# Full-attention layers: a lower cap on side products, a shorter hold on the side bank, and one PSUM read for each bank of keys and queries

## Chip, cores and metric

One core of a Trainium2 chip runs the whole program. The metric is the device time of one execution in microseconds (us). The engines work in parallel and are tied by semaphores: TensorE (PE, matrix products), ScalarE (ACT), VectorE (DVE), GpSimd (POOL), and the queue of SyncE (SP), which issues most DMAs. Products land in banks of PSUM; PE, ACT and DVE reach those banks, POOL works on SBUF only.

## What is computed

Four transformer layers on x of 2048 tokens by 512 features, 32 heads of 16. Layers 0 and 2 attend to a sliding window of 256 keys (weights A), layers 1 and 3 to all 2048 keys, unmasked (weights B):

```python
qkv = (x @ wqkv).reshape(B, S, 3, H, Dh)               # S=2048, H=32, Dh=16
scores = einsum("bhqd,bhkd->bhqk", q, k) * Dh ** -0.5  # A: masked outside 0 <= i-j < 256
o = einsum("bhqk,bhkd->bhqd", softmax(scores), v) @ wo
x = x + A(layernorm(x)); x = x + B(layernorm(x))       # and both once more
```

## The kernel before, in words

**Main work of a full layer.** The layer (1 or 3) has 512 steps. A step is one tile of 128 keys against 512 queries for four heads (`attn_full`). Four groups of eight "quads" of heads and 16 key tiles make 4 x 8 x 16 steps in layer 1; layer 3 runs in the order t (four pairs of quads), c (four chunks of queries), two quads, 16 tiles, so that one (t, c) section has 32 steps. In each step `exps` (L695) issues four score products (L703) into two score tiles and two exponentials on ACT (L707), each over 128x1024. There are three score tiles in PSUM, used in turn. Two steps later `pv` (L747) multiplies the exponentials by the values into the bank `acc[0]`. After the 16 tiles of a quad `epilogue` (L662) has DVE transpose that bank (L670, then short instructions to L687).

**Side work.** Everything else that PE has to do runs as products slipped in after the `pv` of a step: keys and queries of the next chunks or layers (`project`, L472), values (`values`), and the output projection with the residual (`wo`, `wo_part`). In a full layer all of it accumulates in one bank, `acc[1]` (`bank`, L373). A *unit* is one accumulation in that bank: 12 products for a tile of keys, queries, values or `wo`, 12 of half width for half a tile of values, three for `wo_part` (L642). Each product is four 32-column matmuls (L395). PE's instructions are in the order in which Python emits them; the other engines are ordered by the scheduler of the framework, with raised priority where the code says `high_priority`.

**Who decides how much.** `Side.share` (L919) is called once a step, after the `pv`. It adds to `budget`, at least `least` (0.33 or 0.34 in layer 1 and in t = 0, 1 of layer 3; zero later, where the work left over the steps left is what counts), limits it to 0.75, and issues products of 0.222 each while budget, `lag` and the gate allow it. The gate is `clock[0] >= PH["free"]`: `clock` is a planned time that moves by 0.27 for each `exps` (two a step), 1.0 for each `pv`, 0.222 for each product, and by at least 1.8 from step to step. At the end of a unit `mms` (L383) sets `PH["free"]` to the clock plus `after`: 1.6 in general, 2.2 for the units of `project`.

**What follows a unit of keys or queries.** DVE writes the rounded half `sp[:, 0]` (fp16, L508) and the rest `sp[:, 1]` (L509), both from the bank; POOL squares the first half (L514); the SP queue stores both (L519 to L523). When the last unit of the work is done, `keys` or `queries` puts a closure on `pend`: sums of the squares over each head by a product with `hsum` (`squares`, L528, the matmul in L532), again in `acc[1]`, then a maximum (L548) or a scaled copy (L561, L565) by DVE. The next `mms` of any side work empties `pend` first (`settle`, L570), closes the gate for 1.6, and gives the step back. `key_shift` (L575) empties it too, without closing the gate.

Of the kernel before, what the change touches and what calls it, by code (L numbers as in the profile page):

```python
# [9 lines left out]
F32 = mybir.dt.float32  # L10
# [9 lines left out]
P = 128  # L20
NT = S // P
NC = D // P
HT = P // DH
NHT = H // HT
QC = 512
# [6 lines left out]
MM = 0.222  # L32
HEAD_START = 100
EB, XB, XNB, WB, VB, OB = 6, 6, 4, 2, 3, 5
# [155 lines left out]
def fast_path(ctx, tc, flag, a_x, a_wqkv, a_wo, b_wqkv, b_wo, out):  # L190
# [3 lines left out]
    nc = tc.nc  # L194
# [3 lines left out]
    vp = pool("work", 2)  # L198
# [12 lines left out]
    XC, XN, V, O, OT, KM, PH = {}, {}, {}, {}, {}, {}, {"free": 0.0}  # L211
    WT, ST, SP, pend = {}, {}, {}, []

    clock, DONE, XNR, ONR = [0.0], {}, {}, {}
# [6 lines left out]
    def spent(us):  # L221
        clock[0] += us
        return us

    def wait(us):

        return "wait", clock[0] + us
# [124 lines left out]
    def weights(ty, s, n, f0=0, f1=D):  # L352

        for k in ((ty, s), n):
            if k in WT:
                return WT[k].pop() if len(WT[k]) > 1 else WT.pop(k)[0]
        w = wp.tile([P, NC, 2, D], F16, name=f"w{n}", tag="w", bufs=WB)
        if f1 - f0 == D:
            nc.sync.dma_start(w, wd[ty, s])
        else:  # L360
            nc.sync.dma_start(w[:, :, :, :f1 - f0], wd[ty, s][:, :, :, f0:f1])
        return w
# [10 lines left out]
    def bank():  # L373

        if PH["full"]:
            return acc[1]
        turn["bank"] += 1
        PH["extra"] += 1
        if turn["bank"] % 2 and not PH["win"]:
            return ps_s.tile([P, 2, QC], F32, name=f"bs{turn['bank']}", tag="s")[:, 0, :]  # L380
        return PH["pool"].tile([P, QC], F32, name=f"b{turn['bank']}", tag="b")

    def mms(ps, pairs, after=1.6, us=MM, go=True):  # L383


        if PH["full"] and pend:
            settle()
            PH["free"] = clock[0] + 1.6
            yield 0.1
        if PH["win"]:  # L390
            PH["unit"], PH["extra"] = PH["now"], 0
        for i, (a, b) in enumerate(pairs):
            if PH["full"]:
                for g in range(0, P, 32):
                    nc.tensor.matmul(ps[g:g + 32], a[:, g:g + 32], b, start=(i == 0), stop=(i == len(pairs) - 1),  # L395
                                     skip_group_check=True)
            else:
                nc.tensor.matmul(ps, a, b, start=(go and i == 0), stop=(i == len(pairs) - 1))  # L398
            spent(us)
            if i < len(pairs) - 1:  # L400
                if PH["full"]:
                    yield us
                elif i % PH["run"] == PH["run"] - 1:
                    yield PH["run"] * us
            else:
                PH["free"], PH["unit"] = clock[0] + after, None
    TERMS = ((0, 0), (0, 1), (1, 0))
# [64 lines left out]
    def project(l, s, c, act, ht=None, first=False):  # L472


        ty, n = l % 2, f"{l}_{s}_{c}" + ("" if ht is None else f"_h{ht}")
        here = n in WT or (ty, s) in WT
        w = weights(ty, s, n, *((0, D) if ht is None else (ht * P, (ht + 1) * P)))
        yield wait(0 if here else 8)
        xc = XC[l, c]
        if s == 0:  # L480
            dst = rows(qs[ty, c])
        elif ty == 0:
            dst = rows(kw[c])
        else:
            dst = rows(kf)[:, :, c * QC:(c + 1) * QC]
        sqs, begun = {}, []
        if first:
            for t in range(NHT):
                begun.append(bank())
                for k in range(NC):  # L490
                    nc.tensor.matmul(begun[t], w[:, k, 0, t * P:(t + 1) * P], xc[:, 0, k, :], start=(k == 0), stop=False)
                    spent(MM)
        for t in range(NHT) if ht is None else (ht,):
            w0 = t * P if ht is None else 0
            if first:
                ps = begun[t]
                yield from mms(ps, [(w[:, k, a, w0:w0 + P], xc[:, b, k, :]) for a, b in TERMS[1:] for k in range(NC)], go=False)
            else:
                ps = bank()
                yield from mms(ps, [(w[:, k, a, w0:w0 + P], xc[:, b, k, :]) for k in range(NC) for a, b in TERMS], 2.2)  # L500
            settle(not sqs)
            sp = vp.tile([P, 2, QC], F16, name=f"sp{n}_{t}", tag="sp", bufs=4)
            e = 1.0 / UP[s]
            with tc.high_priority(HEAD_START):
                if act:
                    nc.scalar.activation(sp[:, 0], ps, AF.Copy, scale=e)
                else:
                    nc.vector.tensor_scalar(sp[:, 0], ps, e, None, op0=ALU.mult)  # L508
                LAST["DVE"] = nc.vector.scalar_tensor_tensor(sp[:, 1], ps, e, sp[:, 0], op0=ALU.mult, op1=ALU.subtract).ins  # L509
            sq = vp.tile([P, QC], BF16, name=f"sq{n}_{t}", tag="sq", bufs=NHT)  # L510
            if act:
                nc.scalar.activation(sq, sp[:, 0], AF.Square)
            else:
                nc.gpsimd.tensor_tensor(sq, sp[:, 0], sp[:, 0], ALU.mult)  # L514
            sqs[t] = sq

            d = dst[8 * t:8 * t + 8].rearrange("h (d b) n -> (h d) b n", b=4)
            if s:
                nc.sync.dma_start(d[:, 0:2], sp[:, 0:1].broadcast_to([P, 2, QC]))  # L519
                last = nc.sync.dma_start(d[:, 2], sp[:, 1])  # L520
            else:
                nc.sync.dma_start(d[:, 0:2], sp)
                last = nc.sync.dma_start(d[:, 2], sp[:, 0])  # L523
            LAST["SP"] = last.ins
            yield -MM if PH["full"] else -PH["run"] * MM
        return sqs
# [12 lines left out]
    def keys(l, c, act, ht=None, first=False):  # L539
        sqs = yield from project(l, 1, c, act, ht, first)  # L540

        def rest():
            ph = squares(f"k{l}_{c}_{ht}", sqs)
            if l not in KM:
                KM[l] = vp.tile([P, NQ], F32, name=f"km{l}", tag="km", bufs=2)
            r = quarters(ht)
            with tc.high_priority(HEAD_START):
                nc.vector.tensor_reduce(KM[l][r, c:c + 1], ph[r], axis=AX.X, op=ALU.max)  # L548
        pend.append((clock[0] + 3.6, rest, None))
# [20 lines left out]
    def settle(all_=True, most=9):  # L570
        while pend and most and (all_ or pend[0][0] <= clock[0]):
            pend.pop(0)[1]()
            most -= 1
# [13 lines left out]
    def values(l, c, act, halves=(0, 1), tiles=range(4)):  # L587
# [17 lines left out]
        for i in tiles:  # L605
            ps = bank()[:, :D1 - D0]
            yield from mms(ps, [(xc[:, b, k, i * P:(i + 1) * P], w[:, k, a, :D1 - D0]) for k in range(NC) for a, b in TERMS], us=us)
            src = ps.rearrange("p (h d) -> p h d", d=DH)
            for x, h in enumerate(halves if l % 2 else (None,)):
                to = vt[:, i, :, :DH] if h is None else dst[h][:, i, :, :DH]  # L610
                fr = src if h is None else src[:, x * HH:(x + 1) * HH]
                if act:
                    nc.scalar.activation(to, fr, AF.Copy)
                else:
                    LAST["DVE"] = nc.vector.tensor_copy(to, fr).ins  # L615
                one = vt[:, i] if h is None else dst[h][:, i]
                if act:
                    nc.scalar.activation(one[:, :, DH:], one[:, :, :1], AF.Copy, scale=0.0, bias=1.0)
                else:
                    nc.gpsimd.tensor_scalar(one[:, :, DH:], one[:, :, :1], 0.0, 1.0, op0=ALU.mult, op1=ALU.add)  # L620
            yield -us if PH["full"] else -PH["run"] * us
# [228 lines left out]
    class Side:  # L850
# [67 lines left out]

        def share(self):  # L919

            self.budget = min(self.budget + max((self.cost - self.spent) / max(self.steps - 3 - self.k, 1), self.least), 0.75)
            self.lag = max(self.lag - max(0.29, self.least), -0.3)
            while self.q and clock[0] >= PH["free"] and self.budget >= MM / 2 and (self.lag < 0.25 or self.budget > 0.45):
                c = self.one()
                if c is None:
                    break
                self.budget -= abs(c)
                self.lag += abs(c)
# [290 lines left out]
```

## Time and profile before

| | us |
|---|---|
| median of 3 runs (2687.54 to 2692.13) | 2688.03 |
| the profiled execution | 2687.51 |
| its span, first to last instruction | 2685.7 |
| PE busy / ACT busy / DVE busy / POOL busy | 2596.8 / 2390.2 / 844.9 / 580.7 |
| layer 1 (first to last `pv` product) | 454.6 to 1408.8 |
| layer 3 (the same) | 1722.4 to 2671.8 |

The granted clock of PE is 0.995 on average. A busy share says only that an engine had something in flight: both PE and ACT overlap consecutive instructions, so the pitch at which instructions start or end is the measure used below. Rows of the timeline give start, duration, engine, line, operation, tiles, count of merged instructions, and in brackets the idle time before with what ended it.

### The profile page before, as it was taken

Reading aid. Unit: us, or ns where it says so; the run is one execution under the profiler, and the core shown is the slowest. Engines: PE = TensorE matmul, PEld = TensorE weight load, DVE = VectorE, ACT = ScalarE, POOL = GpSimd, SP = SyncE. Lnnn points to the kernel's source line nnn. Section 1 sums busy time; section 2 is a strip of 40 time slices with the busy share of each in tenths; the row PEclk is TensorE's granted clock in tenths of the full one; section 3 lists DMA queues with packets and bytes.
Section 4 is the critical chain, followed back from the end, with each engine's and each line's share of the span. In section 5 each row is a group of like instructions: output and inputs, shape, how many; then the busy total and the mean of one; then the engine's idle time right before and its main releaser. Section 6 shows DMA issues by size and latency. Waiting matters only on the chain.

```text
span 2685.7 us, 59504 instructions
## 1 busy us (share of the span) xinstructions
PE 2596.8 (97%) x24337; PEld 753.9 (28%) x24337; DVE 844.9 (31%) x1937; ACT 2390.2 (89%) x2747; POOL 580.7 (22%) x1203
## 2 busy tenths in 40 slices
PE   8999999999999999999999999999999999999998
PEld 3333344322222222222223333422222222222221
DVE  5746653112232223111216656211222212121111
ACT  5777655999999999999997777699999999999997
POOL 1889750000000000000007777000000000000000
PEclk9999999999999999999999999999999999999999
DMA  6978765223343234222326665423334333333331
GB/s 206 232 219 252 225 204 175 64 95 111 100 101 101 99 111 113 85 68 88 103 76 200 174 182 152 141 82 96 117 123 123 114 106 110 107 101 119 99 93 49
DMA packets 294636, 343.72 MB, mean 128 GB/s; under 512 B 110080, under 2 KB 200672, under 8 KB 289360
## 3 DMA queue, kind: packets, MB, share of 16 engines
q1 hardware_dynamic: 285840, 312.77, 38.8%
q0 software_dynamic: 8512, 27.04, 3.5%
q8 instruction: 193, 3.16, 0.5%
q14 instruction: 91, 0.75, 0.1%
HBM read 228.07 MB, written 96.99 MB: 121 GB/s over the span
## 4 chain that ended last, share of the span: by engine, by line
PE 80%; ACT 8%; DVE 5%; issue 4%; DMA 2%; POOL 1%; SPq 0%; ACTq 0%; DVEq 0%
PE acc L747 31%; PE s L703 21%; PE b L398 11%; PE acc L395 10%; ACT e L707 7%; PE acc L781 5%; PE bs L398 2%; DVE ot L670 1%; DMA wo<-wd 1%; DMA x<-in_A_x_dram 1%; DVE wa L330 0%; DVE sp L509 0%; PE acc L532 0%; DVE xh L437 0%; DVE xh L443 0%
## 5 line engine op out<-in xcount | busy, mean ns | idle before, releaser
L707 ACT ACTIVATE e<-s 128x1024 f32<-128x1024 f32 (+2 forms) x2432 | 2245.5, 1115 | 127.3 <-PE s L703 110.7
L747 PE MATMUL acc<-e,vt 128*17 128x512 f32 x8192 | 1078.8, 598 | 7.9 <-DVE ot L670 6.9
L703 PE MATMUL s<-qt,kt 64*128 64x512 f16 (+3 forms) x5504 | 768.5, 355 | 33.2 <-ACT e L707 16.7
L703 PEld LDWEIGHTS <-kt 64*128 64x128 f16 x5504 | 198.4, 94 | 773.2 <-issue 754.6
L773 POOL TENSOR_SCALAR_AFFINE_SELECT e<-e 128x256 f32<-128x256 f32 x512 | 231.7, 461 | 67.3 <-ACT e L707 66.4
L747 PEld LDWEIGHTS acc<-e,vt 128*17 128x17 f32 x8192 | 136.3, 95 | 387.5 <-issue 352.1
L670 DVE STREAM_TRANSPOSE ot<-acc 128x512 f32<-128x512 f32 x128 | 91.3, 713 | 438.4 <-PE acc L747 324.5
L770 POOL TENSOR_SCALAR_AFFINE_SELECT e<-e 128x256 f32<-128x256 f32 x448 | 198.7, 450 | 50.4 <-ACT e L707 46.2
L781 PE MATMUL acc<-e,vt 128*17 128x384 f32 (+2 forms) x2816 | 195.8, 389 | 0.5 <-POOL e L773 0.5
L687 POOL TENSOR_TENSOR oh<-o,oh 128x512 f16<-128x512 f32 x31 | 36.0, 1163 | 703.6 <-DVE oh L686 703.6
L398 PE MATMUL b<-xc,w 128*128 128x512 f16 x676 | 161.9, 382 | 5.4 <-DVE sp L509 3.7
L514 POOL TENSOR_TENSOR sq_h<-sp_h 128x512 bf16<-128x512 f16 x27 | 28.1, 1041 | 439.2 <-DVE sp_h L508 439.2
L395 PE MATMUL acc<-xc,w_h 128*32 128x512 f16 x1296 | 108.5, 379 | 2.3 <-DVE km L548 2.3
L514 POOL TENSOR_TENSOR sq<-sp 128x512 bf16<-128x512 f16 x28 | 29.1, 1041 | 375.6 <-DVE sp L508 346.0
L395 PE MATMUL acc<-xc,w 128*32 128x512 f16 x1344 | 108.9, 379 | 0.0
L508 DVE TENSOR_SCALAR sp_h<-acc 128x512 f16<-128x512 f32 x27 | 18.6, 690 | 285.4 <-PE acc L395 285.4
L508 DVE TENSOR_SCALAR sp<-acc 128x512 f16<-128x512 f32 x28 | 19.3, 689 | 280.3 <-PE acc L395 270.0
L653 DVE SCALAR_TENSOR_TENSOR x<-acc,x 128x512 f32<-128x512 f32 x60 | 41.5, 692 | 206.9 <-PE acc L395 203.9
L398 PEld LDWEIGHTS <-w 128*128 128x128 f16 x800 | 71.9, 98 | 113.9 <-issue 37.7
L395 PE MATMUL acc<-wo,oh 128*32 128x512 f16 x1296 | 101.3, 379 | 1.3 <-DVE m_None L565 1.3
L615 DVE COPY vt<-acc 128x256 f32<-128x256 f32 (+1 forms) x36 | 18.5, 514 | 258.7 <-PE acc L395 258.7
L395 PE MATMUL acc<-wv,xc 128*32 128x256 f16 (+1 forms) x1728 | 93.2, 308 | 0.2 <-DVE km L548 0.2
(145 smaller groups left out, 1625.8 us busy)
## 6 DMA issues: line engine op xcount, KB each, us to landing
kt<-kf SPq DMA_DIRECT2D x128, 512.0 KB
xd<-x SPq DMA_DIRECT2D x96, 256.0 KB
qt<-qs SPq DMA_DIRECT2D x96, 256.0 KB
x<-xd SPq DMA_DIRECT2D x96, 256.0 KB
w<-wd SPq DMA_DIRECT2D x16, 1024.0 KB
qs<-sp SPq DMA_DIRECT2D x48, 256.0 KB
wo<-wd SPq DMA_DIRECT2D x10, 1024.0 KB
wv<-wd SPq DMA_DIRECT2D x17, 512.0 KB
```

The costliest lines, as they stand in the source:

```text
L395: nc.tensor.matmul(ps[g:g + 32], a[:, g:g + 32], b, start=(i == 0), stop=(i == len(pairs) - 1), skip_group_check=True)
L398: nc.tensor.matmul(ps, a, b, start=(go and i == 0), stop=(i == len(pairs) - 1))
L508: nc.vector.tensor_scalar(sp[:, 0], ps, e, None, op0=ALU.mult)
L514: nc.gpsimd.tensor_tensor(sq, sp[:, 0], sp[:, 0], ALU.mult)
L653: nc.vector.scalar_tensor_tensor(xs[i], ps, 1.0 / (UP[2] * UP[3]), xs[i], op0=ALU.mult, op1=ALU.add)
L670: nc.vector.transpose(ot.rearrange("p b r -> p (b r)"), a)
L703: nc.tensor.matmul(ps[:, h, s0:s0 + wd_], kt[R * h:R * h + R, pr, kc:kc + P], qt[R * h:R * h + R, pr, qc:qc + wd_], start=True, stop=True)
L707: LAST["ACT"] = nc.scalar.activation(e[:, :, w0:w1], ps[:, :, w0:w1], AF.Exp, scale=SCALE).ins
L747: nc.tensor.matmul(a[32 * h:32 * h + DH + 1, :], V[l, qd // 4, j // 8][:, j % 8, 4 * (qd % 4) + h, :], es_[h // 2][:, h % 2, :], start=(j ...
L770: last = nc.gpsimd.affine_select(v, v, pattern=[[0, 2], [-1, P]], compare_op=ALU.is_gt, fill=0.0, base=0, channel_multiplier=1)
L773: last = nc.gpsimd.affine_select(v, v, pattern=[[0, 2], [1, P]], compare_op=ALU.is_ge, fill=0.0, base=0, channel_multiplier=-1)
L781: nc.tensor.matmul(a[32 * h:32 * h + DH + 1, q * P:(q + nb) * P], V[l, (4 * c + j) // 4][:, j % 4, 4 * qd + h, :], es_[h // 2][:, h % 2, s ...
```

## The change

In full layers `share` limits the budget to 0.55 in place of 0.75; every unit closes the gate for 1.45 in place of 1.6 or 2.2, and a `settle` in `mms` as well; and `project` copies the bank into an SBUF tile first (fp32, from the ring of six buffers that also holds x and other 128x512 fp32 tiles), from which L508 and L509 then read. In sliding-window layers the copy is not made, and neither the gate nor the cap is used.

```diff
-    def mms(ps, pairs, after=1.6, us=MM, go=True):
+    def mms(ps, pairs, after=1.45, us=MM, go=True):
         if PH["full"] and pend:
             settle()
-            PH["free"] = clock[0] + 1.6
+            PH["free"] = clock[0] + 1.45
             yield 0.1
...
                 ps = bank()
-                yield from mms(ps, [(w[:, k, a, w0:w0 + P], xc[:, b, k, :]) for k in range(NC) for a, b in TERMS], 2.2)
+                yield from mms(ps, [(w[:, k, a, w0:w0 + P], xc[:, b, k, :]) for k in range(NC) for a, b in TERMS])
             settle(not sqs)
             sp = vp.tile([P, 2, QC], F16, name=f"sp{n}_{t}", tag="sp", bufs=4)
             e = 1.0 / UP[s]
             with tc.high_priority(HEAD_START):
+                if PH["full"]:
+                    out_ps, ps = ps, vp.tile([P, QC], F32, name=f"pr{n}_{t}", tag="x", bufs=XB)
+                    nc.vector.tensor_copy(ps, out_ps)
                 if act:
                     nc.scalar.activation(sp[:, 0], ps, AF.Copy, scale=e)
                 else:
                     nc.vector.tensor_scalar(sp[:, 0], ps, e, None, op0=ALU.mult)
...
         def share(self):
-            self.budget = min(self.budget + max((self.cost - self.spent) / max(self.steps - 3 - self.k, 1), self.least), 0.75)
+            self.budget = min(self.budget + max((self.cost - self.spent) / max(self.steps - 3 - self.k, 1), self.least), 0.55)
```

## The prediction

> **What bounds the kernel now.** I read the page, then the chain of waits, timelines around ends of units, busy time by stretches, and the groups of DVE and POOL.
>
> ```profile
> span 2685.7 us, 59504 instructions
> PE 2596.8 (97%) x24337; PEld 753.9 (28%) x24337; DVE 844.9 (31%) x1937; ACT 2390.2 (89%) x2747; POOL 580.7 (22%) x1203
> 1767.53 1.19 ACT e L707
> ...
> 1774.76 1.29 ACT e L707
> ```
>
> PE and ACT both look full, so their pitches decide. The two chain rows are exponentials from a stretch without side work, eight apart; their ends are 1768.72 and 1776.05, so one takes 7.33 / 8 = 0.916 us and a step (two) 1.833. That is ACT's floor.
>
> ```profile
> 1880.45 0.60 PE L703 MATMUL s<-qt,kt 64*128 64x512 f16 x4
> 1880.56 0.69 DVE L508 TENSOR_SCALAR sp_h<-acc 128x512 f16<-128x512 f32 x1 [8.44 <-PE acc L395]
> 1881.29 0.69 DVE L509 SCALAR_TENSOR_TENSOR sp_h<-acc,sp_h 128x512 f16<-128x512 f32 x1
> 1881.33 1.04 POOL L514 TENSOR_TENSOR sq_h<-sp_h 128x512 bf16<-128x512 f16 x1 [12.96 <-DVE sp_h L508]
> 1881.97 0.60 PE L703 MATMUL s<-qt,kt 64*128 64x512 f16 x4
> 1883.38 0.38 PE L532 MATMUL acc<-sq_h,hsum 128*32 128x512 bf16 x1
> 1883.69 0.60 PE L703 MATMUL s<-qt,kt 64*128 64x512 f16 x4
> 1885.10 0.83 PE L395 MATMUL acc<-wo,oh 128*32 128x512 f16 x12
> 1885.86 0.61 PE L703 MATMUL s<-qt,kt 64*128 64x512 f16 x4
> ```
>
> Here a unit of keys ends at 1880.45, and each L703 row begins a step. A step without side work takes PE 1881.97 - 1880.45 = 1.52; one with the sum of squares 1.72; one with three products (x12) 2.17. So a product is (2.17 - 1.52) / 3 = 0.217, and PE meets ACT's floor at (1.833 - 1.52) / 0.217 = 1.44 products a step. With `least` = 0.33 or 0.34 and 0.222 a product, `share` asks for about 1.5: there PE sets the pace.
>
> ```profile
> core 0: us, PE busy (x) PEld busy (x), PEclk, DMA share, GB/s
> 1958.20:2018.30 60.10, 33.69 (x256) 4.24 (x256) 1.00 0.38 117
> ...
> 2138.40:2199.70 61.30, 33.68 (x256) 4.24 (x256) 1.00 0.36 109
> 2257.70:2316.40 58.70, 33.72 (x260) 4.24 (x256) 1.00 0.34 109
> ```
>
> These stretches hold the L747 matmuls of one (t, c) section of 32 steps each. At t = 1 a section takes 60.1 us: PE's own sum is 32 x 1.52 + 48 products (24 half ones count as 12) x 0.217 + two sums of squares x 0.2 = 59.5. At t = 2 it takes 58.7 = 32 x 1.833: ACT's floor, with PE in reserve. So a PE wait counts in full at t = 1 and c = 2, 3 of t = 0 (six sections) and in most of layer 1, and only beyond the reserve elsewhere.
>
> **The gate, and what it lets through.** At the end of a unit the clock stands at T; the next look comes after two `exps` and a `pv`, at T + 0.54 + 1.0 = T + 1.54 (1.58 after a single product). 1.6 and 2.2 are more, so one step is left empty, as in the rows above; only at the first step of a quad does the clock move further (1.8 + 1.0). 1.45 is less: no step is left empty any more.
>
> Products neither appear nor vanish, so PE's sum stays. Empty steps and steps of three become steps of one and two, and since PE's time is linear in the products, where PE sets the pace this moves nothing. Worked through by hand with `share`'s rules, a section at t = 1 comes out as 7 steps for the 24 half products, 8 for the queries, 1 for squares, 7 for the keys, 1 for squares, 8 for the four short units: 32, just full. Layer 1 ends now with a forced remainder:
>
> ```profile
> 1405.21 1.91 PE L395 MATMUL acc<-wv,xc 128*32 128x512 f16 x32
> 1409.21 5.89 ACT L707 ACTIVATE e<-s 128x768 f32<-128x768 f32 x8 [2.90 <-PE s L703]
> ```
>
> Eight products, and ACT is idle 2.90 us after them. Without empty steps about seven of them find room: -1.5 us.
>
> **The added wait.** When the last unit of keys or queries is done, the next side product first runs the sum of squares, which reads what POOL squared. Before, this came two steps after the unit (above: POOL done at 1882.37, product at 1883.38). After, it comes in the next step. The trace has that case where a unit ends with a quad:
>
> ```profile
> 1866.45 0.61 PE L703 MATMUL s<-qt,kt 64*128 64x512 f16 x4
> ...
> 1868.43 0.38 PE L532 MATMUL acc<-sq_h,hsum 128*32 128x512 bf16 x1 [0.39 <-POOL sq_h L514]
> 1868.73 0.60 PE L703 MATMUL s<-qt,kt 64*128 64x512 f16 x4
> 1869.22 1.02 ACT L707 ACTIVATE e<-s 128x1024 f32<-128x1024 f32 x1 [0.25 <-PE s L703]
> ```
>
> PE waits about 0.4 us for the square, ACT starves. Behind PE's wait stand the next step's scores, for which ACT waits. The change lengthens the way to the square by the copy:
>
> ```profile
> L615 DVE COPY vt<-acc 128x512 f32<-128x512 f32 x11 | 7.6, 692 | 117.1 <-PE acc L395 117.1
> L437 DVE TENSOR_SCALAR xn<-x,mv,y 128x512 f32<-128x512 f32 x12 | 6.4, 537 | 0.3
> L686 DVE CAST oh<-o 128x512 f16<-128x512 f32 x15 | 6.4, 427 | 0.5
> L443 DVE TENSOR_TENSOR xh<-xn,xh 128x512 f16<-128x512 f32 x12 | 8.2, 686 | 0.1
> ```
>
> The copy costs 0.69 (L615), as long as L508 did; L508 from SBUF then takes 0.43 to 0.54 (L686, L437; taken 0.48), plus 0.03 of gap. The square comes 0.51 later, so the wait in the next step is 0.4 + 0.51 = 0.91 where there was none, and 0.51 more where there were 0.4. If DVE's reads from SBUF gained nothing, 0.69, it would be 1.1; if the scheduler put PE's look later, 0.
>
> How often:
>
> ```profile
> L532 PE MATMUL acc<-sq,hsum 128*32 128x512 bf16 x28 | 3.9, 382 | 0.1
> L532 PE MATMUL acc<-sq_h,hsum 128*32 128x512 bf16 x27 | 10.2, 378 | 2.3 <-POOL sq_h L514 2.3
> PEld L532 <- DVE sp L509: 2.8, 3, 1.0
> PE acc L532 <- POOL sq_h L514: 2.3, 6, 0.4
> ```
>
> Layer 1 has 28 / 4 = 7 such sums, layer 3 27. The last two rows are waits, of layer 1 and of the first half of layer 3: three and six sums stand in the next step already. The six PE-bound sections of layer 3 have two sums each, one of either kind: 6 x (0.91 + 0.51) = 8.5. Layer 1: 4 x 0.91 + 3 x 0.51 = 5.2, of which I count 3.5, since it also has stretches with fewer than 1.44 products a step. The other 15 of layer 3 stand in sections at the floor: when PE is blocked on a score tile, ACT has three exponentials ahead, 2.75 us; PE needs 1.52 - 0.217 = 1.3 for the rest of the step, 0.2 for the sum and 0.49 from scores to exponential (1868.73 to 1869.22), so the reserve is about 0.8; 15 x 0.1 = 1.5.
>
> At c = 3 `key_shift` empties `pend` and opens the gate at once:
>
> ```profile
> 1929.65 0.61 PE L395 MATMUL acc<-xc,w_h 128*32 128x512 f16 x8 [0.78 <-DVE km L548]
> 1930.69 5.84 ACT L707 ACTIVATE e<-s 128x1024 f32<-128x1024 f32 x6 [1.64 <-PE s L703]
> ```
>
> PE waits for the square, then for DVE's maximum, and ACT idles 1.64. This stays, 0.51 longer; two of the three are counted above, the third (t = 2) adds 0.5.
>
> **The rest.** Within a work the next unit may start 1.41 us after the last (1881.97 to 1883.38 is scores and `pv`). The bank is free after 0.1 + 0.69, so 0.6 is left; with L508 and L509 both on the bank (0.1 + 1.4) there would be 0.1 of wait. An epilogue on DVE in that gap eats it: +0.5 in all. DVE gains 55 copies of 0.69, 38 us in 1910 us where it is a quarter busy: off the path. SP's stores come 0.5 later; behind them stand the loads of the next quad, issued some 30 us ahead: nothing, or at most 0.5 per unit without that cover. The copies share the ring of six with x: four x and two copies per section, so a buffer comes round after about 59 us: nothing; were it held, DVE would wait with the epilogue behind it.
>
> Sum: 8.5 + 3.5 + 1.5 + 0.5 + 0.5 - 1.5 = +13.0. The profiled execution, 2687.51 (span 2685.7 and 1.8 around it), becomes 2700.5; it lies 0.5 under the median 2688.03, so I forecast 2701.
>
> **Rivals.** *Slower still.* L509 would read two SBUF tiles just as POOL reads one for the square. Before, L509 has one source in PSUM. If DVE, which starts 0.04 earlier (1881.29 against 1881.33), kept POOL out for its 0.69 (L443), the square would come 0.65 later again: 19 sums x 0.65 = 12.4, and the 15 at the floor, whose reserve is used up, 15 x 0.65 = 9.8: 2701 + 22 = 2723.
>
> ```profile
> L443 DVE TENSOR_TENSOR xh<-xn,xh 128x512 f16<-128x512 f32 x20 | 15.9, 794 | 0.7 <-ACT xh L440 0.4
> ```
>
> For it: the same L443 takes 0.794 in the stage between the full layers, where POOL masks, against 0.686 in layer 1. Against: 0.11 is far from a whole instruction. The Trainium skill, "SBUF — State Buffer", section "Who interferes with whom", states that a DVE instruction with two SBUF inputs contends with a GpSimd instruction that reads SBUF, and that whoever issues first blocks the other fully; the trace agrees in direction, not in size.
>
> *Faster.* The three score tiles cover the wait for the square in the PE-bound stretches too, and even steps feed ACT better.
>
> ```profile
> ACT e L707 <- PE s L703: 6.8, 11, 1.3
> ACT e L707 <- PE s L703: 6.2, 12, 1.6
> ACT e L707 <- PE s L703: 0.7, 1, 0.7
> ```
>
> In layer 1, the first and the second half of layer 3 ACT waits 13.7 us visibly for scores; half of that and the 1.5 at layer 1's end make -8: 2680. It decides from the point where ACT has more than 0.91 us of scores ahead at the end of a unit. Against: where a unit ends with a quad today, a wait of 0.39 starves ACT at once.
>
> *No change.* The waits are covered as in the last case, but nothing is won, since PE's products are the same: 2688. So also if the looks don't move into the next step.
>
> **Numbers.** Forecast case 0.47 (its own range 2694 to 2710: waits of 0.6 to 1.1), slower still 0.20, no change 0.17, faster 0.16. The bound is 0.2%, 5.4 us. A twentieth of the forecast case may come out under +5.4. Slower 0.65, same 0.19, faster 0.16. The range goes from 2682 (most of the faster case outside) to 2724 (above it the contended case with L508 unimproved).
>
> **What would show it.** Right: L532 in every case one step after its unit, waiting about 0.9 us on POOL; at t = 1 sections of 61.5 us, at t = 2 still 58.7; L395 rows of at most x8; no x32 at layer 1's end. POOL's L514 at 1.7 or starting after L509 would show the contention. Wrong: ACT's idle time in full layers below 13.7 us, or L532 without waits.

## The result, and the profile after

The kernel after the change takes 2729.86 us (median of 4 runs, 2727.59 to 2731.45) against 2688.07 before: a ratio of 1.0152, 95% interval 1.0139 to 1.0165. It is 41.8 us slower. The forecast was 2701, 13 us slower, with a range up to 2724: the sign was right, the size three times too small, and the time outside the range.

The page after, and the stretches from the first to the last `pv` product of layers 1 and 3. In the second and third fence the columns are the stretch, its length, PE's busy time on that line with its count, the same for weight loads, PE's clock, DMA share and GB/s. The copy adds three lines, so L703 is now L706, L707 L710, L747 L750, L532 L535, L514 L517; L507 is the copy, L511 the rounded half, L512 the rest.

```profile
span 2725.8 us, 59617 instructions
PE 2600.2 (95%) x24337; PEld 747.2 (27%) x24337; DVE 870.0 (32%) x1992; ACT 2394.5 (88%) x2747; POOL 601.4 (22%) x1203
```

Before:

```profile
454.60:1408.80 954.20, 538.66 (x4096) 68.06 (x4096) 1.00 0.31 93
1722.40:2671.80 949.40, 540.11 (x4096) 68.24 (x4096) 1.00 0.33 102
```

After, with one (t, c) section of t = 1, 2 and 3 below:

```profile
455.90:1416.40 960.50, 540.01 (x4096) 68.19 (x4096) 1.00 0.31 92
1727.50:2711.90 984.40, 541.82 (x4096) 68.34 (x4096) 1.00 0.32 100
1973.30:2035.90 62.60, 33.69 (x256) 4.25 (x256) 1.00 0.35 111
2286.70:2348.00 61.30, 33.73 (x260) 4.24 (x256) 1.00 0.34 104
2531.50:2591.20 59.70, 33.76 (x260) 4.25 (x256) 1.00 0.31 96
```

Of the span's 40.1 us, 35.0 lie in layer 3 (984.4 - 949.4) and 6.3 in layer 1; the rest of the program is 1.2 shorter. PE runs the same 24337 matmuls. In layer 3 the sections of t = 1 went from 60.1 to 62.6 and, against the forecast, those of t = 2 from 58.7 to 61.3: the sections with PE to spare lost as much as those without. (About 1.6 us of layer 3 is another matter: in one section PE's granted clock was 0.97 in the mean, and it took 65.1 where its twin took 63.5.)

The timeline after, at the end of a unit of queries in t = 2:

```profile
2303.65 0.61 PE L706 MATMUL s<-qt,kt 64*128 64x512 f16 x4
2303.76 0.69 DVE L507 COPY pr_h<-acc 128x512 f32<-128x512 f32 x1 [10.22 <-PE acc L395]
2304.49 0.43 DVE L511 TENSOR_SCALAR sp_h<-pr_h 128x512 f16<-128x512 f32 x1
2304.95 0.69 DVE L512 SCALAR_TENSOR_TENSOR sp_h<-pr_h,sp_h 128x512 f16<-128x512 f32 x1
2305.06 1.48 POOL L517 TENSOR_TENSOR sq_h<-sp_h 128x512 bf16<-128x512 f16 x1 [10.28 <-DVE sp_h L511]
2306.59 0.38 PE L535 MATMUL acc<-sq_h,hsum 128*32 128x512 bf16 x1 [1.35 <-POOL sq_h L517]
2306.90 0.61 PE L706 MATMUL s<-qt,kt 64*128 64x512 f16 x4
2307.39 4.81 ACT L710 ACTIVATE e<-s 128x1024 f32<-128x1024 f32 x5 [0.95 <-PE s L706]
```

The sum of squares now stands one step after its unit, as forecast. PE waits 1.35 us for the square, the scores behind it come late, and ACT idles 0.95. Two rows of this chain are new: the copy, and a square of 1.48 us in place of 1.04, which runs beside L512. Over the program, waits and groups:

```profile
PE acc L535 <- POOL sq_h L517: 35.3, 26, 1.7
PE acc L535 <- POOL sq L517: 7.2, 6, 1.4
L517 POOL TENSOR_TENSOR sq_h<-sp_h 128x512 bf16<-128x512 f16 x27 | 40.0, 1480 | 466.9 <-DVE sp_h L511 466.9
```

26 of layer 3's 27 sums wait, 35.3 us in all (2.3 before), and six of layer 1's seven, 7.2. Together 42.5 of waiting beside 40.1 of span.

### The profile page after: what moved, and what is told of

Its sections match the earlier page's. It is cut to its first block, busy times and chain, and to the rows that moved or that the text cites. A ratio compares the mean times of both kernels' runs of the same rounds, so it can differ in the third digit from the quotient of the medians.

```text
span 2725.8 us, 59617 instructions
## 1 busy us (share of the span) xinstructions
PE 2600.2 (95%) x24337; PEld 747.2 (27%) x24337; DVE 870.0 (32%) x1992; ACT 2394.5 (88%) x2747; POOL 601.4 (22%) x1203
## 4 chain that ended last, share of the span: by engine, by line
PE 77%; ACT 7%; DVE 7%; issue 4%; DMA 2%; POOL 2%; SPq 0%; ACTq 0%; POOLq 0%; DVEq 0%
PE acc L750 30%; PE s L706 20%; PE b L398 10%; PE acc L395 10%; ACT e L710 7%; PE acc L784 5%; PE bs L398 1%; POOL sq_h L517 1%; DVE ot L673 1%; DVE pr_h L507 1%; DMA wo<-wd 1%; DMA kt<-kf 1%; PE acc L535 0%; DVE xh L443 0%; DVE sp_h L511 0%
## 5 line engine op out<-in xcount | busy, mean ns | idle before, releaser
L710 ACT ACTIVATE e<-s 128x1024 f32<-128x1024 f32 (+2 forms) x2432 | 2249.9, 1094 | 164.3 <-PE s L706 149.8
L750 PE MATMUL acc<-e,vt 128*17 128x512 f32 x8192 | 1081.9, 600 | 5.2 <-DVE ot L673 3.0
L706 PE MATMUL s<-qt,kt 64*128 64x512 f16 (+3 forms) x5504 | 766.9, 356 | 33.3 <-ACT e L710 16.4
L706 PEld LDWEIGHTS <-kt 64*128 64x128 f16 x5504 | 190.7, 94 | 793.2 <-issue 775.4
L750 PEld LDWEIGHTS acc<-e,vt 128*17 128x17 f32 x8192 | 136.6, 95 | 398.3 <-issue 365.6
L517 POOL TENSOR_TENSOR sq_h<-sp_h 128x512 bf16<-128x512 f16 x27 | 40.0, 1480 | 466.9 <-DVE sp_h L511 466.9
L517 POOL TENSOR_TENSOR sq<-sp 128x512 bf16<-128x512 f16 x28 | 41.4, 1480 | 373.4 <-DVE sp L511 372.9
L395 PE MATMUL acc<-wo,oh 128*32 128x512 f16 x1296 | 111.7, 379 | 0.0
L507 DVE COPY pr_h<-acc 128x512 f32<-128x512 f32 x27 | 18.6, 691 | 286.8 <-PE acc L395 286.8
L656 DVE SCALAR_TENSOR_TENSOR x<-acc,x 128x512 f32<-128x512 f32 x60 | 41.4, 690 | 205.6 <-PE acc L395 199.6
L507 DVE COPY pr<-acc 128x512 f32<-128x512 f32 x28 | 19.3, 689 | 241.9 <-PE acc L395 241.9
```

What stands on the lines that cost most here:

```text
L507: nc.vector.tensor_copy(ps, out_ps)
L656: nc.vector.scalar_tensor_tensor(xs[i], ps, 1.0 / (UP[2] * UP[3]), xs[i], op0=ALU.mult, op1=ALU.add)
L706: nc.tensor.matmul(ps[:, h, s0:s0 + wd_], kt[R * h:R * h + R, pr, kc:kc + P], qt[R * h:R * h + R, pr, qc:qc + wd_], start=True, stop=True)
L710: LAST["ACT"] = nc.scalar.activation(e[:, :, w0:w1], ps[:, :, w0:w1], AF.Exp, scale=SCALE).ins
L750: nc.tensor.matmul(a[32 * h:32 * h + DH + 1, :], V[l, qd // 4, j // 8][:, j % 8, 4 * (qd % 4) + h, :], es_[h // 2][:, h % 2, :], start=(j ...
```

## The experiments

The theories, as the expectations name them. **W**: the loss is PE's wait for POOL's square one step after the last unit of a work, and every such microsecond counts. **C**: the loss comes from the cap, which hinders catching up. **D**: it is DVE's extra copies. **P**: the square is slower because L512 reads two SBUF tiles beside it. **R**: the remainder of side work forced at the end of layer 1 costs time. The ratios are against runs of the kernel before that were taken on the same chip together with them.

| kernel | median us | before | ratio (95% interval) |
|---|---|---|---|
| gate_only | 2703.67 | 2688.82 | 1.0049 (1.0032 to 1.0065) |
| copy_only | 2700.39 | 2688.82 | 1.0047 (1.0030 to 1.0064) |
| hold_last | 2687.52 | 2688.82 | 0.9999 (0.9989 to 1.0008) |
| rest_from_bank | 2723.07 | 2688.82 | 1.0128 (1.0111 to 1.0145) |
| cap_back | 2732.07 | 2689.91 | 1.0160 (1.0144 to 1.0175) |
| half_first | 2699.12 | 2689.91 | 1.0040 (1.0024 to 1.0055) |
| before_hold | 2686.31 | 2689.91 | 0.9992 (0.9983 to 1.0001) |
| hold_cap_back | 2690.15 | 2689.91 | 1.0003 (0.9994 to 1.0012) |
| hold_shift | 2683.01 | 2689.57 | 0.9976 (0.9966 to 0.9985) |
| hold_shift_short | 2678.50 | 2689.57 | 0.9953 (0.9940 to 0.9967) |

### hold_last: the change, with the wait taken out

```diff
-                yield from mms(ps, [... TERMS])
+                yield from mms(ps, [... TERMS], 3.0 if ht is not None or t == NHT - 1 else 1.45)
```

> The kernel after the change, but the last unit of each piece of keys or queries closes the gate for 3.0, so that its sum of squares comes two steps later even where a quad ends (1.45 stays for all other units, with copy and cap). W: no L535 waits for POOL, layer 3 falls from 988 to about 950 us, layer 1 keeps its forced remainder: 2688 to 2693 us. C and D: 2725 or more, since copy and cap are still there.

Layer 3 from first to last `pv`, and what is left of the wait (an idle time of 0.2 in the group of L535):

```profile
1719.10:2668.80 949.70, 540.39 (x4096) 68.19 (x4096) 1.00 0.34 104
L535 PE MATMUL acc<-sq_h,hsum 128*32 128x512 bf16 x27 | 10.2, 378 | 0.2 <-POOL sq_h L517 0.2
```

With copy, cap and the slower square all in place the time is that of the kernel before. C and D fall; W holds: the loss is where the sum of squares stands.

### gate_only and copy_only: the parts alone

gate_only has only the three numbers of `after` changed; copy_only only the copy.

> The gate of 1.45 for every unit and every settle, without the copy and with the old cap. Theory W (the lost time is PE waiting for POOL's square one step after the last unit of keys or queries, and each such wait costs its whole length): the wait is 0.4 us, as it was where a unit ended with a quad; 20 more such waits in layer 3 make +8, layer 1 adds 2 to 4, so 2696 to 2700 us. Theory C (the lost time is lost catching up: the cap of 0.55 leaves too much side work for the end of a layer): close to before, 2686 to 2690. Theory D (DVE's 55 extra copies are the loss): 2688.

> The copy alone, with the old gate and the old cap. W: only the nine sums of squares that already stand in the step after their unit, where a unit ends with a quad, wait longer, 1.35 in place of 0.4: 9 x 0.95 = +8.6, so about 2697 us. D: the whole loss, 2720 or more. C: 2688.

The waits for the square, gate_only and then copy_only:

```profile
PE acc L532 <- POOL sq_h L514: 9.4, 25, 0.4
```

```profile
PE acc L535 <- POOL sq_h L517: 8.3, 7, 1.4
PE acc L535 <- POOL sq L517: 3.5, 3, 1.2
```

Neither part is free: the gate alone makes 25 waits of 0.4, the copy alone makes nine long ones of 1.1 to 1.4, where a unit ends with a quad (the tenth is 0.2). D's price for copy_only, 2720, is refuted. Both expectations of W were short by 3 us or more. In copy_only the excess lies in layer 1, which grew by 6.3 us where three longer waits were priced at 2.9. In gate_only layer 3 grew by 9.2 and layer 1 by 4.3, near their prices; 3.1 us of the profiled execution lie outside both layers, where the gate is not used. The parts multiply: the gate sets how many sums wait, the copy how long; 0.49% and 0.47% apart, 1.52% together.

### rest_from_bank and half_first: the way to the square

```diff
-                LAST["DVE"] = nc.vector.scalar_tensor_tensor(sp[:, 1], ps, e, ...
+                LAST["DVE"] = nc.vector.scalar_tensor_tensor(sp[:, 1], out_ps if PH["full"] else ps, e, ...
```

> The kernel after the change, but the rest (L512) is computed from the PSUM bank instead of the SBUF copy, so that DVE has one SBUF input while POOL squares. Theory P (POOL's square grows from 1.04 to 1.48 us because L512 reads two SBUF tiles beside it): the square is back at 1.04, the wait falls from 1.35 to 0.91, 32 x 0.44 = 14 us less: about 2716 us. Without P: the square stays at 1.48 and the time at 2730.

half_first moves the copy behind the rounded half, which is then written from the bank:

```diff
-                if PH["full"]:
-                    out_ps, ps = ps, vp.tile([P, QC], F32, ...)
-                    nc.vector.tensor_copy(ps, out_ps)
                 if act:
...
                     nc.vector.tensor_scalar(sp[:, 0], ps, e, None, op0=ALU.mult)
+                if PH["full"]:
+                    out_ps, ps = ps, vp.tile([P, QC], F32, ...)
+                    nc.vector.tensor_copy(ps, out_ps)
```

> The kernel after the change, but the rounded half is written from the bank first, and the copy follows; the rest is then computed from the copy. As many DVE instructions, the bank held 1.4 us in place of 0.7. Theory W (what counts is the way to the square): POOL starts 0.5 us earlier and is disturbed only in its last third, the wait falls from 1.35 to 0.4 to 0.6, layer 3 from 988 to 963 to 967 us, layer 1 gains waits of 0.1 between units: 2705 to 2710 us. If the number of DVE instructions or the moment of the bank's release were what counts: 2730 or more.

rest_from_bank: the square's group, the wait, and the waits of layer 1 between units of one work:

```profile
L517 POOL TENSOR_TENSOR sq_h<-sp_h 128x512 bf16<-128x512 f16 x27 | 28.0, 1039 | 465.6 <-DVE sp_h L511 465.6
PE acc L535 <- POOL sq_h L517: 23.8, 26, 1.3
PE acc L395 <- DVE sp L512: 11.3, 21, 1.7
```

P holds: with one SBUF input beside it the square is back at 1.04 and 26 waits make 23.8 us, 0.92 each. Layer 3 fell by 13.8 (984.4 to 970.6), of which 1.6 is the slower clock of one section after the change; 26 x 0.44 = 11.4 was expected of it. The total fell by less than the 14 expected, as I had not counted that the bank is now held through three DVE instructions: in layer 1 the 21 transitions within a work wait 11.3 us for it.

half_first, at the end of a unit:

```profile
2283.02 0.68 DVE L511 COPY pr_h<-acc 128x512 f32<-128x512 f32 x1
2283.18 1.04 POOL L517 TENSOR_TENSOR sq_h<-sp_h 128x512 bf16<-128x512 f16 x1 [9.76 <-DVE sp_h L508]
2283.73 1.03 DVE L512 SCALAR_TENSOR_TENSOR sp_h<-pr_h,sp_h 128x512 f16<-128x512 f32 x1
2284.28 0.38 PE L535 MATMUL acc<-sq_h,hsum 128*32 128x512 bf16 x1 [0.39 <-POOL sq_h L517]
```

As many DVE instructions, in another order (here L508 is the rounded half and L511 the copy), and of the loss of 41.8 us against the kernel before 9.2 are left (2699.12 against 2689.91). It was less than expected: the wait is 0.4, the low end, and layer 3 takes 956.5 in place of 963 to 967. Here POOL issues first and keeps its 1.04; now it is L512 that takes 1.03 in place of 0.69. In these two orders the one that issues first goes undisturbed, and the other loses 0.34 or 0.44 us.

### Does every microsecond of wait count?

Layer 3's length beside its waits for the square, one pair from each trace: before 949.4 with 2.3, hold_last 949.7 with 0.2, copy_only 956.0 with 8.3, half_first 956.5 with 9.4, gate_only 958.6 with 9.4, rest_from_bank 970.6 with 23.8, after 984.4 with 35.3. Against before the length grows by 6.6, 7.1, 9.2, 21.2 and 35.0 us for 6.0, 7.1, 7.1, 21.5 and 33.0 us of added wait (1.6 of the 35.0 is the slower clock). The same section of t = 2 in gate_only and rest_from_bank:

```profile
2271.10:2330.60 59.50, 33.71 (x260) 4.23 (x256) 1.00 0.33 103
```

```profile
2287.60:2347.90 60.30, 33.61 (x260) 4.24 (x256) 1.00 0.34 106
```

Two waits of 0.4, 0.9 and 1.35 make 58.7 into 59.5, 60.3 and 61.3: they cost 0.8, 1.6 and 2.6 for 0.8, 1.8 and 2.7 of wait, nearly the whole of it, in sections that ran at ACT's floor without it. In hold_last, which differs from the kernel after the change by the hold alone, such a section takes 58.7 again. Only t = 3, with 0.75 products a step, swallows something: one wait of 1.26 costs 1.0 there, and one of 0.29 (gate_only) nothing.

### cap_back and hold_cap_back: the cap

cap_back is the change with 0.75 in place of 0.55, hold_cap_back is hold_last with the same.

> The kernel after the change with the cap of the budget back at 0.75. Theory R (the cap leaves side work over at the end of layer 1, which then runs in one piece while ACT is idle 6.65 us, where it was 2.90): ACT's idle time there falls to about 1.5 us, as with the gate alone, the waits for POOL's square stay at 1.35: 2724 to 2726 us. If the cap has nothing to do with it: 2730.

> The last unit of each piece of keys or queries closes the gate for 3.0, all others for 1.45, with the copy, and the cap back at 0.75. W and R together: no waits for POOL's square, ACT's idle time at the end of layer 1 at 1.5 us in place of 7.4: about 5 us under the same with the cap of 0.55, 2681 to 2683 us. R wrong: 2687.

The end of layer 1 after the change, and ACT there in cap_back:

```profile
1408.95 2.13 PE L395 MATMUL acc<-wv,xc 128*32 128x512 f16 x36
1411.87 2.77 PE L395 MATMUL acc<-wv,xc 128*32 128x512 f16 x48 [0.79 <-DVE vt L618]
1416.73 5.89 ACT L710 ACTIVATE e<-s 128x768 f32<-128x768 f32 x8 [6.65 <-PE s L706]
```

```profile
1418.87 1.51 ACT L710 ACTIVATE e<-s 128x768 f32<-128x768 f32 x2 [1.46 <-PE s L706]
```

The cap does make the remainder: 21 products (84 matmuls) in one piece and 6.65 us of idle ACT with 0.55, none and 1.46 with 0.75. But R falls. Layer 1 takes 960.5 with the remainder and 962.6 without, and the times did not fall: the ratios are 1.0160 beside 1.0152, and 1.0003 beside 0.9999 for hold_cap_back and hold_last, with intervals that overlap. The same products, run earlier, lengthened the steps that took them: the last three stretches of 32 steps in layer 1 take 59.4, 58.4 and 63.4 us with the remainder and 60.4, 60.7 and 60.7 without.

The cap has a price elsewhere. In hold_last four sections of layer 3 wait 0.8 us each for DVE's L656 and take 60.6; without the cap (hold_cap_back) those waits are gone, and such sections take 59.6. The medians of the two kernels do not show this.

### before_hold, hold_shift and hold_shift_short: a version from what was found

before_hold is the kernel before with the hold of 3.0 after the last unit (2.2 elsewhere). hold_shift adds

```diff
         key_shift(l, ht)
+        PH["free"] = clock[0] + 1.45
         yield -1e-6
```

and hold_shift_short also has 1.45 for the units of values and of the output projection and after a `settle`; none has the copy.

> The kernel before the change with one edit: the last unit of each piece of keys or queries closes the gate for 3.0 in place of 2.2, so that the sum of squares comes two steps later even where a quad ends. W: the nine waits of 0.4 go (3.6 us), and of the three places where the maximum of the keys is taken at once the wait for the square, not that for DVE; 2682 to 2685 us. If those waits were covered: 2688.

> The kernel before the change with the last unit of each piece of keys or queries closing the gate for 3.0, and with the gate closed for 1.45 after the maximum of the keys is taken (key_shift), so that the next unit does not wait for DVE there. W: three waits of about 0.8 us for DVE and what they cost go too; the three sections with key_shift fall from 61 to 59.7 us, 3 to 4 us under the hold of 3.0 alone (2686): 2682 to 2683 us. If such waits are covered: 2686.

> The same, and the gate of 1.45 for the units of values and of the output projection and after each settle (2.2 between units of keys and queries, no copy, cap 0.75). If steps without side work cost time (the aim of a shorter gate), 2 to 5 us less than the former: 2678 to 2681 us. W: PE's sum is the same, so no difference from the former beyond 2 us.

In before_hold no L532 waits for POOL, but the next unit still waits for the maximum, and the result cannot be told from 1 (its interval ends at 1.0001); 2686.31 lies between W's price and none:

```profile
PE acc L395 <- DVE km L548: 3.5, 3, 1.3
```

hold_shift takes these away too. A section with `key_shift` at t = 1, before_hold and then hold_shift:

```profile
2137.40:2198.50 61.10, 33.69 (x256) 4.25 (x256) 1.00 0.36 104
```

```profile
2134.80:2194.50 59.70, 33.69 (x256) 4.23 (x256) 1.00 0.39 108
```

hold_shift_short is the fastest of all: 0.9953, an interval wholly below 1. Its shorter gate is the part of the change that does no harm, since no sum of squares moves by it. The medians of hold_shift and hold_shift_short differ by 4.5 us: W's bound of 2 did not hold, and the other price, 2 to 5, did. The two profiled executions, 2681.28 and 2678.50, differ by 2.8, and the layers account for that (layer 3 944.0 to 942.4, layer 1 953.9 to 952.6); the rest is that hold_shift's profiled execution lay 1.7 under its median. A section at t = 1 gives only some 0.1 of it (59.7 to 59.6). Which steps give the 2.9 was not isolated.

## Why the prediction was wrong

**Right: the mechanism and the sign.** The gate's arithmetic held: the sum of squares moved into the next step in all but two cases, where no side product came for 7 and 18 us after the square. The wait for POOL was named, and W was then shown by taking it out alone (hold_last).

**Wrong: the reserve.** This is the step that failed most. The prediction gave the 15 sums in sections at ACT's floor a reserve of 0.8 us, and so 0.1 of loss each, 1.5 in all. Layer 3 outside the six PE-bound sections lost about 19 us, some 1.3 for each sum. 0.8 is what PE has when it is blocked on a score tile, and at the end of a unit it did not have that. ACT's row in the timeline after shows what was there: the exponential before the idle time ends at 2306.44 and the fifth behind it at 2312.20, which is 5.76 us for 5 x 0.916 = 4.58. So 1.18 of the 1.35 was lost within five exponentials (0.95 of it is idle time, the rest shows only in the ends), and the reserve at that place was under 0.2. At t = 3, with fewer products, it was 0.3: waits of 0.29, 0.81 and 1.26 cost 0, 0.5 and 1.0 (gate_only, rest_from_bank, after). Why so little was left at t = 2 is argued, not isolated: the steps of two products take 1.95 against ACT's 1.833, so those before the sum have been living on the reserve, and those behind it find none. That nearly the whole wait is paid at t = 2 is shown.

**Wrong in size: the wait.** Forecast 0.91, measured 1.35. The copy (0.69) and the half from SBUF (0.43, forecast 0.48) came as estimated, and rest_from_bank shows the sum without contention, 0.92. The missing 0.44 is the rival that I gave 0.20: L512 with two SBUF inputs. I argued against it with the 0.11 by which another DVE instruction grew beside POOL's masks; that row is an average of single instructions between 0.68 and 0.90 and could not tell what one full overlap costs. The Trainium skill, "SBUF — State Buffer", section "Who interferes with whom", says that the one that issues first blocks the other fully. Both orders are in the traces: L512 first, the square grows by 0.44; the square first, L512 grows by 0.34. Its order rule agrees; each is somewhat less than the whole overlap (0.58 and 0.49). The six sections lost 15.8 us for a forecast of 8.5: the larger wait is 12 x 0.44 = 5.3 of the difference, the slower clock 1.6.

**Wrong: the end of layer 1.** Forecast -1.5, since the remainder would find room. It grew instead, from 8 products to 21. With no empty steps `lag` holds the work at three products in two steps, and a budget that never passes 0.55 can't override it for a second product; the working by hand did not include that. cap_back showed no gain in layer 1's length without the remainder. Layer 1 as a whole lost 6.3 for a forecast of 3.5 - 1.5 + part of 0.5, and its waits are 7.2.

**The rivals.** Slower still was the nearest (2723 for 2730), for the reason that it gave. That it came so near is partly luck: it kept the 1.5 for the first 0.91 us of the 15 sums, which is too little, and priced the blocking at 0.65 each where 0.44 came, which is too much. Faster and no change were refuted by the time and by L535's waits.

## What to carry to other kernels

When an instruction is moved earlier in an in-order queue, look at what it reads, not only at what the move frees: here the bank was free in time, but the next instruction in line needed the end of a chain through two other engines. An engine's spare time over a stretch is not its reserve at a given moment: read it off the timeline at the very place, by how much later the next instructions end behind a known wait, since idle time alone shows too little of the loss. And leveling work on an engine that already sets the pace bought little here; what cost or won most was its waits.

## What was not expected of the hardware

L512, with two SBUF sources, and POOL's square, which reads SBUF, did not run side by side at full speed: the later one took 0.34 (L512, 0.69 to 1.03) or 0.44 us (the square, 1.04 to 1.48) longer, the earlier one lost nothing. Where L512 had one source in PSUM (rest_from_bank), and beside the copy from PSUM into SBUF (half_first), POOL kept its 1.04.
